# Linear attention, a Fourier mix and an MLP on one core: every engine's order written by a list scheduler of the kernel's own

## The chip, the cores and the metric

The kernel runs on one core of a Trainium2 chip. A core has five engines that run at the same time, each taking its own instructions strictly in the order in which they stand: TensorE (PE, matmuls), VectorE (DVE), ScalarE (ACT), GpSimd (POOL) and SyncE (SP, which here only issues transfers). Engines wait for one another through semaphores; transfers run on 16 DMA engines that all queues share. The metric is the device time of one execution in microseconds, as the median of several runs.

## The reference

Inputs are r, k, v of 4 batches x 8 heads x 768 steps x 48, a decay w and a bonus u of 8 x 48, and two MLP weights. The output is 4 x 768 x 384 in float32.

```python
for t in range(S):                       # linear attention, per batch and head
    cur = u*k_t (outer) v_t
    y_t = r_t @ (state + cur)
    state = w*state + k_t (outer) v_t
x = y, heads side by side                # (4, 768, 384)
mixed = real(fft(fft(x, axis=1), axis=2))
u = x + mixed
un = (u - mean(u)) / sqrt(var(u) + 1e-06)
out = u + relu(un @ w_ch1) @ w_ch2       # 384 -> 1536 -> 384
```

## The kernel before

A batch has six chunks of 128 steps, so there are 24 chunks (numbered 0 to 23), one Fourier transform a batch, and 8 half batches of 384 rows (hf 0 to 7) for the MLP.

**A chunk** takes three phases. `phase1`: k and r (tile kr) times powers of the decay give KR on DVE; v is cast to V on ACT; PE turns KR (eight transposes into tp), ACT copies that to KRT, and DVE multiplies its halves into PR. `phase2`: eight score matmuls A_ps; the triangle mask gives MA, either by a cast AC on ACT and a select on POOL, or by one multiplication on DVE; u_ps is the state's update, which DVE scales into Sst. `phase3`: yd_ps collects the bonus, the state's part and the chunk's own part; ACT copies the bonus out (DE), POOL multiplies it with V (TT), DVE adds the two into X.

**A batch** whose X is complete is folded by `fold` (EO, XF on DVE) and transformed by `fourier`: 18 matmuls over time (L298) whose results ACT casts into TT2 (called TT in the trace's rows, L300), DVE reverses them into TR, then six blocks of six matmuls over columns (L316 to L320), to which DVE adds X (UF) and of which it takes mean and variance (st, MV). ACT takes the root (rstd), DVE inverts it and makes nm, ACT writes the normed rows UN, and a transposing DMA on SP's queue turns them into UNT (L339). The MLP is `mlp1` (12 pieces of three matmuls and a Relu on ACT into HT) and `mlp2` (three pieces of twelve matmuls, the addition osb on DVE, and the output's DMA issued by POOL). All of this shares eight PSUM banks, three of them the ring "mm" of the transforms and the MLP.

**The order** is that of a hand-written loop over 26 steps: it calls phase1 of chunk s, phase2 of chunk s - 1, phase3 of chunk s - 2, and between them steps the transform in hand (`advance`) and takes from the list M of MLP pieces (`feed`). The framework's own scheduler then moves instructions on each engine by its estimates, except those held by `keep_in_program_order` (all of SP's). Six chunks of inputs are loaded ahead; the tables te, to and hid come behind them. W1 and W2 are loaded by POOL's queue after the TT of chunks 2 and 6 (`marks`).

Of the kernel before, what the change touches and what calls it, by code (L numbers as in the profile page):

```python
# [9 lines left out]
AluOp = mybir.AluOpType  # L10
# [16 lines left out]
def _tables():  # L27
# [31 lines left out]
    return [np.ascontiguousarray(x.astype(bf)) for x in (te, to, hid, mtri, ident)]  # L59


@with_exitstack
def kernel(
# [106 lines left out]

    def load(i):
        b, q = divmod(i, NQ)
        sl = slice(q * 128, (q + 1) * 128)
        kr = inp.tile([128, 2, H, D], F32, name="kr")
        vt = inp.tile([128, H, D], F32, name="vt")
        sp(nc.sync.dma_start(out=kr[:, 0], in_=k[b, :, sl, :].rearrange("h p d -> p h d")))  # L176
        sp(nc.sync.dma_start(out=kr[:, 1], in_=r[b, :, sl, :].rearrange("h p d -> p h d")))
        if i == 0:
            sp(nc.sync.dma_start(out=ident, in_=id_c.ap()))
        sp(nc.sync.dma_start(out=vt, in_=v[b, :, sl, :].rearrange("h p d -> p h d")))  # L180
        if i == 0:
            sp(nc.sync.dma_start(out=mtri, in_=mtri_c.ap()))
        chk[i]["in"] = (kr, vt)


    def phase1(i):
        c = chk[i]
        kr, vt = c["in"]
        KR = KRs[i % NB]
        nc.vector.tensor_tensor(  # L190
            out=KR.rearrange("t s p (a d) -> t (s p) a d", a=2)[:, :, :, 0:D],
            in0=kr.rearrange("t s (p a) d -> t (s p) a d", a=2),
            in1=wtab.rearrange("t s (p a d) -> t (s p) a d", a=2, d=D), op=AluOp.mult)
        V = wp.tile([128, H, D], BF16, name="V", bufs=4)
        cv = nc.scalar.copy(V, vt)  # L195
        if i == 0:
            tc.keep_in_program_order(cv)
        tp = ps.tile([128, 2, NP, 128], BF16, name="tp", bufs=1)
        for s in range(2):
            for p in range(NP):  # L200
                nc.tensor.transpose(tp[:, s, p, :], KR[:, s, p, :], ident)  # L201
        KRT = wp.tile([128, 2, NP, 128], BF16, name="KRT", bufs=4)
        nc.scalar.copy(KRT, tp)  # L203
        PR = wp.tile([128, NP, 128], BF16, name="PR", bufs=4)
        nc.vector.tensor_tensor(out=PR, in0=KRT[:, 0], in1=KRT[:, 1], op=AluOp.mult)  # L205
        c.update(KR=KR, V=V, KRT=KRT, PR=PR)

    def phase2(i):
        b, q = divmod(i, NQ)
        c = chk[i]  # L210
        KR, V, KRT = c["KR"], c["V"], c["KRT"]
        A_ps = [ps.tile([128, NP, 128], F32, name="A_ps", bufs=2) for _ in range(2)]
        for p in range(NP):
            for a in range(2):
                rows = slice(a * 64, a * 64 + 64)
                nc.tensor.matmul(A_ps[a][:, p, :], lhsT=KRT[rows, 0, p, :], rhs=KRT[rows, 1, p, :],  # L216
                                 start=(p == 0), stop=(p == NP - 1), skip_group_check=True)
        MAs = []
        for a in range(2):
            MA = wp.tile([128, NP, 128], BF16, name="MA", bufs=6)  # L220
            if a == 0 and b > 0:
                nc.vector.tensor_tensor(out=MA, in0=A_ps[a], in1=mtri.unsqueeze(1).to_broadcast([128, NP, 128]),
                                        op=AluOp.mult)
            else:
                AC = wp.tile([128, NP, 128], BF16, name="AC", bufs=2)
                nc.scalar.copy(AC, A_ps[a])  # L226
                nc.gpsimd.affine_select(out=MA, in_=AC, pattern=[[0, NP], [1, 128]], base=0,  # L227
                                        channel_multiplier=-1, compare_op=AluOp.is_gt, fill=0.0)
            MAs.append(MA)
        S = c.get("S")  # L230
        if q < NQ - 1:
            u_ps = ps.tile([128, NP, 2, D], F32, name="u_ps", bufs=1)
            for p in range(NP):
                nc.tensor.matmul(u_ps[:, p, :, :], lhsT=KR[:, 0, p, :], rhs=V[:, 2 * p:2 * p + 2, :],
                                 start=(p == 0), stop=(q == 0 and p == NP - 1), skip_group_check=True)
            if q > 0:
                nc.tensor.matmul(u_ps, lhsT=ident, rhs=S, start=False, stop=True, skip_group_check=True)
            Sn = wp.tile([128, NP, 2, D], BF16, name="Sst", bufs=4)
            nc.vector.tensor_tensor(out=Sn, in0=u_ps, in1=WD, op=AluOp.mult)
            chk[i + 1]["S"] = Sn  # L240
        c["MA"] = MAs
# [215 lines left out]
```

## Time and profile before

| | |
|---|---|
| runs | 235.19 us median of 3 (232.9 to 235.21) |
| the profiled execution | 235.22 us; its span, from first to last instruction, 233.5 us |
| busy share of the span | PE 82%, DVE 56%, ACT 55%, POOL 27% |
| TensorE's granted clock, mean | 0.931 of full speed |
| read from memory | 20.32 MB, of which k, r, v in pieces of 192 bytes |

The profile page divides the span into 40 equal slices and gives each engine's busy tenths in each. PE's line reads 2 to 9 with dips; the DMA line reads 9 from the second to the 16th slice and little behind that. A busy PE is not a PE at its peak: its durations double when its clock is at the lower level, and a row of the page does not say what an instruction waits for in a queue.

### The profile page before, as it was taken

How to read it: one execution, taken by the hardware profiler on the slowest of the kernel's cores; microseconds unless marked ns; L12 is line 12 of the kernel's file. 1: busy time of each engine (PE TensorE's matmuls, PEld its weight loads, DVE VectorE, ACT ScalarE, POOL GpSimd, SP SyncE). 2: the span in 40 equal slices, each digit the busy share in tenths (PEclk: the TensorE clock that was granted, in tenths of full speed). 3: DMA queues.
4: the chain of work that ended last, by engine and by line, in shares of the span. 5: the costliest groups of instructions: out<-in, count | busy, mean ns of one | idle time of the engine just before them, and what ended most of it. 6: DMA issues, size and time to landing. Idle time of an engine off the chain costs nothing.

```text
span 233.5 us, 4269 instructions
## 1 busy us (share of the span) xinstructions
PE 191.2 (82%) x1640; PEld 122.3 (52%) x1640; DVE 131.1 (56%) x273; ACT 129.3 (55%) x261; POOL 64.1 (27%) x93
## 2 busy tenths in 40 slices
PE   0289856991798979987999789964999999999990
PEld 0156634670555645665565456652565565566660
DVE  4367479795955694598881454782841277101020
ACT  4677534734798675577247564543356637654500
POOL 4038944701213441343100133162001000101021
PEclk9999999999599988995599999995699999999998
DMA  5999999999999996101603940102003103310111
GB/s 108 187 188 197 284 206 186 181 190 190 175 177 166 208 182 137 36 0 36 121 34 66 210 70 10 36 34 53 0 34 84 36 34 86 84 70 35 67 70 67
DMA packets 88917, 25.33 MB, mean 108 GB/s; under 512 B 85312, under 2 KB 86976, under 8 KB 88896
## 3 DMA queue, kind: packets, MB, share of 16 engines
q1 hardware_dynamic: 85216, 17.96, 44.7%
q0 software_dynamic: 3680, 7.08, 11.8%
q8 instruction: 13, 0.21, 0.4%
q14 instruction: 8, 0.07, 0.1%
HBM read 20.32 MB, written 4.72 MB: 107 GB/s over the span
## 4 chain that ended last, share of the span: by engine, by line
issue 29%; PE 22%; ACT 11%; DMA 11%; POOL 9%; DVE 8%; SPq 6%; POOLq 0%; ACTq 0%; DVEq 0%
PE mm L353 6%; PE mm L362 5%; DMA vt<-in_v_dram 5%; DMA kr<-in_r_dram 5%; POOL TT L264 4%; POOL out_dram L367 3%; ACT KRT L203 3%; PE tp L201 3%; ACT HT L355 2%; ACT UN L337 2%; POOL MA L227 2%; SPq L176 2%; PE mm L298 2%; PE A_ps L216 2%; DMA UNT<-UN 2%
## 5 line engine op out<-in xcount | busy, mean ns | idle before, releaser
L355 ACT ACTIVATE HT<-mm 128x384 bf16<-128x384 f32 x96 | 46.0, 497 | 35.1 <-PE mm L353 34.7
L353 PE MATMUL mm<-UNT,W 128*128 128x384 bf16 x288 | 59.2, 341 | 2.7 <-DMA UNT<-UN 1.7
L362 PE MATMUL mm<-W,HT 128*128 128x384 bf16 x288 | 51.4, 331 | 0.0
L353 PEld LDWEIGHTS <-W 128*128 128x128 bf16 x288 | 28.3, 101 | 21.2 <-issue 4.8
L362 PEld LDWEIGHTS <-HT 128*128 128x128 bf16 x288 | 28.6, 99 | 19.5 <-issue 1.6
L365 DVE TENSOR_TENSOR osb<-mm,UF 128x384 f32<-128x384 f32 x24 | 13.4, 557 | 43.2 <-PE mm L362 43.1
L367 POOL DMA_DIRECT2D out_dram<-osb x24 | 13.3, 555 | 87.9 <-DVE osb L365 87.9
L227 POOL TENSOR_SCALAR_AFFINE_SELECT MA<-AC 128x512 bf16<-128x512 bf16 x30 | 22.2, 751 | 40.1 <-ACT AC L226 35.5
L264 POOL TENSOR_TENSOR TT<-V,DE 128x384 bf16<-128x384 bf16 x24 | 22.6, 941 | 36.4 <-ACT DE L262 34.2
L190 DVE TENSOR_TENSOR KR<-kr,wtab 128x768 bf16<-128x768 f32 x24 | 23.7, 991 | 12.9 <-DMA kr<-in_r_dram 12.9
L201 PE MATMUL tp<-ident,KR 128*128 128x128 bf16 x192 | 20.0, 258 | 12.3 <-DVE KR L190 11.5
L203 ACT COPY KRT<-tp 128x1024 bf16<-128x1024 bf16 x24 | 24.3, 1012 | 7.7 <-PE tp L201 7.3
L201 PEld LDWEIGHTS <-KR 128*128 128x128 bf16 x192 | 15.0, 116 | 15.4 <-DVE KR L190 13.4
L216 PE MATMUL A_ps<-KRT 64*128 64x128 bf16 x192 | 15.4, 257 | 9.0 <-ACT KRT L203 4.4
L226 ACT CAST AC<-A_ps 128x512 bf16<-128x512 f32 x30 | 17.2, 592 | 9.9 <-PE A_ps L216 9.8
L271 DVE TENSOR_TENSOR X<-yd_ps,TT 128x384 bf16<-128x384 f32 x24 | 13.3, 553 | 14.8 <-POOL TT L264 14.4
L195 ACT CAST V<-vt 128x384 bf16<-128x384 f32 x24 | 12.4, 515 | 12.6 <-POOL TT L264 6.6
L300 ACT CAST TT<-mm 128x386 bf16<-128x386 f32 (+1 forms) x24 | 14.1, 603 | 5.6 <-PE mm L298 5.5
L337 ACT ACTIVATE UN<-UF,nm,rstd 128x384 bf16<-128x384 f32 x24 | 15.2, 697 | 3.6 <-DVE nm L333 3.5
L216 PEld LDWEIGHTS <-KRT 64*128 64x128 bf16 x192 | 8.5, 108 | 15.5 <-issue 7.4
L205 DVE TENSOR_TENSOR PR<-KRT 128x512 bf16<-128x512 bf16 x24 | 11.3, 471 | 8.5 <-ACT KRT L203 8.4
L269 PE MATMUL yd_ps<-V,MA 128*128 128x48 bf16 x192 | 11.0, 199 | 5.3 <-ACT DE L262 3.5
(64 smaller groups left out, 239.7 us busy)
## 6 DMA issues: line engine op xcount, KB each, us to landing
kr<-in_k_dram SPq DMA_DIRECT2D x24, 192.0 KB, 4.6
kr<-in_r_dram SPq DMA_DIRECT2D x24, 192.0 KB, 4.6
vt<-in_v_dram SPq DMA_DIRECT2D x24, 192.0 KB, 4.7
out_dram<-osb POOLq DMA_DIRECT2D x24, 192.0 KB, 2.2
W<-in_moe_w_ch_dram POOLq DMA_DIRECT2D x6, 384.0 KB, 7.6
hid_t<-hid_c SPq DMA_DIRECT2D x1, 576.0 KB, 5.7
te_t<-te_c SPq DMA_DIRECT2D x1, 289.5 KB, 4.8
to_t<-to_c SPq DMA_DIRECT2D x1, 288.0 KB, 4.5
```

Of the source, the lines that this page charges most:

```text
L190: nc.vector.tensor_tensor(out=KR.rearrange("t s p (a d) -> t (s p) a d", a=2)[:, :, :, 0:D], in0=kr.rearrange("t s (p a) d -> t (s p) a d" ...
L201: nc.tensor.transpose(tp[:, s, p, :], KR[:, s, p, :], ident)
L203: nc.scalar.copy(KRT, tp)
L216: nc.tensor.matmul(A_ps[a][:, p, :], lhsT=KRT[rows, 0, p, :], rhs=KRT[rows, 1, p, :], start=(p == 0), stop=(p == NP - 1), skip_group_check ...
L226: nc.scalar.copy(AC, A_ps[a])
L227: nc.gpsimd.affine_select(out=MA, in_=AC, pattern=[[0, NP], [1, 128]], base=0, channel_multiplier=-1, compare_op=AluOp.is_gt, fill=0.0)
L264: marks[i] = nc.gpsimd.tensor_tensor(out=TT, in0=V, in1=DE.unsqueeze(2).to_broadcast([128, H, D]), op=AluOp.mult)
L337: nc.scalar.activation(out=UN[:, j, :], in_=UF[:, j, :], func=Act.Identity, scale=rstd[:, j:j + 1], bias=nm[:, j:j + 1])
L353: nc.tensor.matmul(hp, lhsT=W1[:, dt, ft * 128:(ft + 1) * 128], rhs=UNT[:, :, dt, :], start=(dt == 0), stop=(dt == 2))
L355: nc.scalar.activation(out=HTs[hf][:, ft, :], in_=hp, func=Act.Relu)
L362: nc.tensor.matmul(op, lhsT=HTs[hf][:, ft, j * 128:(j + 1) * 128], rhs=W2[:, ft, :], start=(ft == 0), stop=(ft == 11))
L367: nc.gpsimd.dma_start(out=out[b, row:row + 128, :], in_=osb)
```

## The change

The loop, `feed` and `advance` go. In their place every operation (a group of matmuls, a cast, a DMA) is declared with an engine, a duration in nanoseconds, what it reads and writes, and a priority; `_Schedule.order` then plays a clock over them, always taking next the operation that can start first, with rings of buffers and one serial DMA pipe among the conditions; and `emit` writes the instructions in that order, which `manual_schedule` keeps. The operations themselves stay, with these exceptions.

- The normed rows of batch 0 are turned by PE (18 transposes against ident into the ring mm) and copied to UNT by DVE; batches 1 to 3 keep the DMA.
- kr and vt have rings of 4 buffers where they had 6, AC 3 where it had 2.
- Chunk 5 too has one of its masks on DVE now, and a chunk's POOL mask is made ahead of its DVE mask.
- `mlp2` is two operations of six matmuls, between which others may stand. W1 and W2 are issued behind the start of TT of chunks 3 and 7.

The diff, cut to its core (what was a loop body is the same instruction inside `op`):

```diff
+    LATENCY = 80
+    LANDING = 1900
+    COLD = 42000
...
+        def room(o):
+            t = 0.0
+            taken = {}
+            for tl in o["new"]:
+                ring = rings.setdefault(tl.ring, [])
+                n = len(ring) + taken.get(tl.ring, 0) - tl.bufs
+                taken[tl.ring] = taken.get(tl.ring, 0) + 1
+                if n >= 0:
+                    if n >= len(ring):
+                        return None
+                    for p in ring[n].ops:
+                        if "end" not in p:
+                            return None
+                        t = max(t, p["end"])
...
+            for e, ops in cand.items():
+                at = free.get(e, 0.0)
+                pick = None
+                for o in ops:
+                    t = room(o)
+                    if t is None:
+                        continue
+                    start = max(at, o["ready"], t + self.LATENCY)
+                    key = (start, o["pri"], o["n"])
+                    if pick is None or key < pick[0]:
+                        pick = (key, o)
+                if pick and (best is None or pick[0] < best[0]):
+                    best = pick
+            assert best, "no operation can start"
+            (start, _, _), o = best
+            cand[o["eng"]].remove(o)
+            ns = o["ns"] * (1.9 if o["eng"] == "PE" and start < self.COLD else 1)
+            end = start + ns
+            free[o["eng"]] = end
+            if o["dma"]:
+                dma_free = max(dma_free, end) + o["dma"]
+                end = dma_free + self.LANDING
+            o["start"], o["end"] = start, end
+            for tl in o["new"]:
+                rings[tl.ring].append(tl)
+            done.append(o)
...
+        c["kr"] = kr = new(inp, [128, 2, H, D], F32, "kr", 4)
+        c["vt"] = vt = new(inp, [128, H, D], F32, "vt", 4)
+        op("SP", 600, lambda: nc.sync.dma_start(out=kr()[:, 0], in_=k[b, :, sl, :].rearrange("h p d -> p h d")),
+           w=[("k", i)], new=[kr], dma=1030, pri=10 * i - 50)
...
+        op("ACT", 510, lambda: nc.scalar.copy(V(), vt()), r=[("v", i), "wtab"], w=[("V", i)], new=[V], use=[vt], pri=pri + 1)
...
+            if a == 0 and i >= NQ - 1:
...
+        for a in (1, 0):
+            mask(a)
...
+            if b == 0:
+                for j in range(3):
+                    turned(sh, j, UN, UNT)
+                op("NONE", 0, lambda: None, r=[("UNT", b, sh, j) for j in range(3)], w=[("UNT", b, sh)])
+                return
+            op("SP", 1200, lambda: nc.sync.dma_start_transpose(
+                out=UNT().rearrange("p j c t -> p (j c) t"), in_=UN().rearrange("p j d -> p (j d)")),
+               r=[("UN", b, sh, j) for j in range(3)], w=[("UNT", b, sh)], new=[UNT], use=[UN], dma=1500, pri=-1000)
+
+        def turned(sh, j, UN, UNT):
+            tq = new(ps, [128, 3, 128], BF16, "mm", 3)
+
+            def mm():
+                for dt in range(3):
+                    nc.tensor.transpose(tq()[:, dt, :], UN()[:, j, dt * 128:(dt + 1) * 128], ident)
+
+            op("PE", 200, mm, r=[("UN", b, sh, j)], w=[("tq", sh, j)], new=[tq], use=[UN], pri=pri + 1 + sh)
+            op("DVE", 450, lambda: nc.vector.tensor_copy(UNT()[:, j, :, :], tq()), r=[("tq", sh, j)],
+               w=[("UNT", b, sh, j)], new=[UNT] if j == 0 else [], use=[tq, UNT],
+               after=[("UNT", b, sh, 0)] if j else [], pri=-100)
+
+        for sh in range(2):
+            UF = new(bp, [128, 3, DM], F32, "UF", 5)
+            UNT = new(bp, [128, 3, 3, 128], BF16, "UNT", 5)
...
+        op("PE", 985, lambda: mm(0, 6), r=[("HT", hf, ft) for ft in range(6)] + ["W2"], w=[("mo", hf, j, 0)], new=[mo],
+           use=[HT], pri=pri)
+        op("PE", 985, lambda: mm(6, 12), r=[("HT", hf, ft) for ft in range(6, 12)] + [("mo", hf, j, 0)],
+           w=[("mo", hf, j)], use=[HT, mo], pri=pri)
...
+    weights("W1", lambda n: w1[n * 128:(n + 1) * 128, :], lambda n: W1[:, n, :], [("TT", 3)])
+    weights("W2", lambda n: w2[n * 512:(n + 1) * 512, :].rearrange("(f p) d -> p f d", p=128),
+            lambda n: W2[:, n * 4:(n + 1) * 4, :], [("TT", 7)])
...
+    with tc.manual_schedule():
+        sch.emit()
```

Three places show what the scheduler makes of it. In the rows a name's number tells one buffer from another.

ACT at the start of the program, before and then after; lw, wtab, lwc and wdec are the tables of the decay's powers, V the cast of chunk 0 (vt_122, vt_127 its input), KRT the copy of its turned rows:

```order
L113 ACTIVATE lw_90<-wrow_71 128x384
L116 ACTIVATE wtab_92<-lw_90,icol_77 128x384
L115 ACTIVATE wtab_92<-lw_90,ncol_79 128x384
L118 ACTIVATE lwc_95<-wuc_81 128x4
L120 ACTIVATE wdec_97<-lwc_95 128x4
L121 ACT_TABLE_LOAD
L195 CAST V_157<-vt_122 128x384
L203 COPY KRT_168<-tp_159 128x1024
```

```order
L239 ACTIVATE lw_90<-wrow_71 128x384
L319 CAST V_143<-vt_127 128x384
L242 ACTIVATE wtab_92<-lw_90,icol_77 128x384
L241 ACTIVATE wtab_92<-lw_90,ncol_79 128x384
L244 ACTIVATE lwc_95<-wuc_81 128x4
L246 ACTIVATE wdec_97<-lwc_95 128x4
L247 ACT_TABLE_LOAD
L327 COPY KRT_165<-tp_146 128x1024
```

The cast of chunk 0's v, which followed the tables and the second table load, now stands ahead of wtab.

ACT from the last casts TT2 of batch 0's transform to its first normed rows, before and then after; V_631, V_781 and V_894 are the casts of chunks 8 to 10, V_654 and V_678 those of chunks 8 and 9, AC, DE and KRT belong to chunks 7 to 9, rstd and UN to the half batch hf 0:

```order
L300 CAST TT2_651<-mm_693 128x2x192
L195 CAST V_631<-vt_367 128x384
L300 CAST TT2_651<-mm_699 128x386
L203 COPY KRT_642<-tp_633 128x1024
L300 CAST TT2_651<-mm_704 128x2x192
L195 CAST V_781<-vt_439 128x384
L226 CAST AC_860<-A_ps_848 128x512
L262 COPY DE_880<-yd_ps_871 128x8
L195 CAST V_894<-vt_512 128x384
L203 COPY KRT_792<-tp_783 128x1024
L330 ACTIVATE rstd_770<-MV_736,eps_t_88 128x3
L337 ACTIVATE UN_775<-UF_734,nm_773,rstd_770 128x384 x3
```

```order
L467 CAST TT2_633<-mm_525 128x386
L319 CAST V_654<-vt_395 128x384
L467 CAST TT2_633<-mm_646 128x2x192
L467 CAST TT2_633<-mm_657 128x386
L319 CAST V_678<-vt_464 128x384
L467 CAST TT2_633<-mm_668 128x2x192
L327 COPY KRT_701<-tp_680 128x1024
L350 CAST AC_786<-A_ps_767 128x512
L398 COPY DE_798<-yd_ps_777 128x8
L521 ACTIVATE rstd_810<-MV_726,eps_t_88 128x3
L327 COPY KRT_812<-tp_788 128x1024
L530 ACTIVATE UN_823<-UF_722,nm_817,rstd_810 128x384 x3
```

Before, the casts of chunks 9 and 10 and one KRT stand between the last TT2 and rstd; now the casts of chunks 8 and 9 stand among the TT2, and ahead of rstd there is one KRT and no cast, with another KRT between rstd and UN.

DVE behind the transform of batch 1, up to nm of hf 2, before and then after; UF, st and MV lead to rstd and nm of hf 2 and hf 3, osb is the MLP's output, the rest (X, PR, MA, Sst) is attention:

```order
L326 BN_AGGR MV_1517<-st_1561 128x2
L205 TENSOR_TENSOR PR_1627<-KRT_1625 128x512
L325 BN_STATS st_1594<-UF_1515 128x6
L222 TENSOR_TENSOR MA_1668<-A_ps_1658,mtri_74 128x512
L326 BN_AGGR MV_1517<-st_1594 128x2
L239 TENSOR_TENSOR Sst_1680<-u_ps_1674,WD_100 128x384
L331 RECIPROCAL rstd_1597<-rstd_1597 128x3
L271 TENSOR_TENSOR X_1357<-yd_ps_1714,TT_1725 128x384
L333 SCALAR_TENSOR_TENSOR nm_1600<-MV_1517,rstd_1597 128x3
```

```order
L505 TENSOR_TENSOR UF_1624<-mm_1626,X_659 128x2x192
L510 BN_STATS st_1666<-UF_1529 128x6
L512 BN_AGGR MV_1578<-st_1666 128x2
L510 BN_STATS st_1678<-UF_1624 128x6
L512 BN_AGGR MV_1692<-st_1678 128x2
L510 BN_STATS st_1696<-UF_1624 128x6
L523 RECIPROCAL rstd_1690<-rstd_1690 128x3
L602 TENSOR_TENSOR osb_1706<-mm_1668,UF_756 128x384
L525 SCALAR_TENSOR_TENSOR nm_1708<-MV_1578,rstd_1690 128x3
```

Before, three attention operations (MA, Sst, X) stand between the last st of hf 2 and its nm; now one osb of the MLP does, and two st of hf 3.

## Rows read from the trace of the kernel before

**Rows 1.** Timeline: start, duration, engine, line; first MLP matmuls (PE), last addition (DVE).

```profile
63.73 1.16 PE L353 MATMUL mm<-UNT,W 128*128 128x384 bf16 x3
...
228.30 0.56 DVE L365 TENSOR_TENSOR osb<-mm,UF 128x384 f32<-128x384 f32 x1 [1.39 <-PE mm L362]
```

**Rows 2.** Waiting chain in order of time: start, duration; matmul groups at the full clock.

```profile
76.30 1.95 PE mm L362 x12
...
147.80 0.33 PE A_ps L216 x8
...
152.95 0.46 PE tp L201 x8
```

**Rows 3.** PE's groups from 63.7 on: line, shapes, count, busy us, mean ns.

```profile
L201 PE MATMUL tp<-ident,KR 128*128 128x128 bf16 x104 | 9.5, 228 | 1.0 <-ACT KRT L203 0.6 <-DVE KR L190 0.3
```

**Rows 4.** Windows of 4 us: busy PE, PEld, DVE, ACT, POOL; PEclk; DMA share, GB/s.

```profile
60.00:64.00 4.00, 3.42 (x39) 2.37 (x37) 3.55 (x8) 2.74 (x7) 1.42 (x2) 0.50 0.88 163
...
104.00:108.00 4.00, 2.41 (x27) 1.78 (x28) 3.74 (x10) 3.13 (x6) 1.79 (x3) 0.74 0.00 2
108.00:112.00 4.00, 3.38 (x45) 2.66 (x42) 3.47 (x6) 2.73 (x7) 2.15 (x3) 0.50 0.50 92
112.00:116.00 4.00, 3.86 (x20) 2.17 (x17) 2.92 (x6) 0.49 (x1) 0.28 (x1) 0.50 0.73 136
...
156.00:160.00 4.00, 1.12 (x22) 0.90 (x19) 2.07 (x5) 2.54 (x5) 1.53 (x3) 0.64 0.00 0
160.00:164.00 4.00, 2.38 (x25) 1.44 (x22) 1.49 (x3) 0.17 (x1) 1.44 (x2) 0.50 0.41 78
164.00:168.00 4.00, 4.00 (x20) 2.35 (x19) 3.50 (x7) 1.47 (x3) 0.00 (x0) 0.58 0.00 0
```

**Rows 5.** ACT's timeline from 44 to 64 us; in brackets idle time and what ended it.

```profile
55.04 0.51 ACT L195 CAST V<-vt 128x384 bf16<-128x384 f32 x1 [3.16 <-DMA vt<-in_v_dram]
...
56.36 0.30 ACT L330 ACTIVATE rstd<-MV,eps_t 128x3 f32<-128x3 f32 x1
57.62 1.90 ACT L337 ACTIVATE UN<-UF,nm,rstd 128x384 bf16<-128x384 f32 x3 [0.96 <-DVE nm L333]
```

**Rows 6.** DVE's timeline: the third mean and variance of hf 0.

```profile
52.88 0.17 DVE L326 BATCH_NORM_AGGREGATE MV<-st 128x2 f32<-128x6 f32 x1
```

**Rows 7.** SP's timeline (issue of the first transposing DMA) and tile UNT's landing times.

```profile
59.55 1.39 SPq L339 DMA_TRANSPOSE UNT<-UN  x1
...
DMA to landing us min/median/max: 3.2/3.4/4.7
```

**Rows 8.** Groups by line: reversing copy and addition on DVE, 128 partitions.

```profile
L322 DVE TENSOR_TENSOR UF<-mm,X 128x384 f32<-128x384 f32 x24 | 13.0, 547 | 3.2 <-PE mm L320 3.1
...
L302 DVE COPY TR<-TT 128x768 bf16<-128x768 bf16 x12 | 4.8, 402 | 8.0 <-ACT TT L300 7.9
```

**Rows 9.** Timeline: chunk 9's v, issued by SP, and batch 0's last TT2 cast.

```profile
41.40 0.83 SPq L180 DMA_DIRECT2D vt<-in_v_dram  x1
...
47.33 0.62 ACT L300 CAST TT<-mm 128x384 bf16<-128x384 f32 x1
```

**Rows 10.** DMA, three issues of v (4.56, 41.40, 44.22 us): KB, us to landing.

```profile
vt<-in_v_dram SPq DMA_DIRECT2D x1, 192.0 KB, 3.6
...
vt<-in_v_dram SPq DMA_DIRECT2D x1, 192.0 KB, 6.4
...
vt<-in_v_dram SPq DMA_DIRECT2D x1, 192.0 KB, 10.7
```

**Rows 11.** Timelines of ACT and DVE at the program's start.

```profile
5.22 0.61 ACT L116 ACTIVATE wtab<-lw,icol 128x384 f32<-128x384 f32 x1
...
7.09 0.96 DVE L190 TENSOR_TENSOR KR<-kr,wtab 128x768 bf16<-128x768 f32 x1 [3.28 <-DMA kr<-in_r_dram]
```

**Rows 12.** DVE's timeline behind batch 1's transform, and PE's first matmuls of hf 2.

```profile
106.29 0.47 DVE L333 SCALAR_TENSOR_TENSOR nm<-MV,rstd 128x3 f32<-128x3 f32 x1
...
112.79 1.12 PE L353 MATMUL mm<-UNT,W 128*128 128x384 bf16 x3
```

More of the change, by code (lines that the diff above doesn't have):

```diff
@@ L181, in load @@
         if i == 0:
[L182 to L206, printed above, removed]
@@ L208, in phase2, with attend @@
-    def phase2(i):
+            op("SP", 400, lambda: nc.sync.dma_start(out=mtri, in_=mtri_c.ap()), w=["mtri"], dma=100, pri=-46)
+    def attend(i):
         b, q = divmod(i, NQ)
         c = chk[i]
[L211 to L229, printed above, removed]
@@ new lines, in attend, with scores @@
+        op("DVE", 410, lambda: nc.vector.tensor_tensor(out=PR(), in0=KRT()[:, 0], in1=KRT()[:, 1], op=AluOp.mult),
+           r=[("KRT", i)], w=[("PR", i)], new=[PR], use=[KRT], pri=pri + 1)
+        A_ps = [new(ps, [128, NP, 128], F32, "A_ps", 2) for _ in range(2)]
+        MA = [new(wp, [128, NP, 128], BF16, "MA", 6) for _ in range(2)]
+        def scores():
+            for p in range(NP):
+                for a in range(2):
+                    rows = slice(a * MASKROWS, (a + 1) * MASKROWS)
+                    nc.tensor.matmul(A_ps[a]()[:, p, :], lhsT=KRT()[rows, 0, p, :], rhs=KRT()[rows, 1, p, :],
+                                     start=(p == 0), stop=(p == NP - 1), skip_group_check=True)
@@ new lines, in first @@
+                y = yd()[:, 0:DM].rearrange("t (h d) -> t h d", h=H)
+                for p in range(NP):
+                    nc.tensor.matmul(y[:, 2 * p:2 * p + 2, :], lhsT=KRT()[:, 1, p, :], rhs=S()[:, p, :, :],
+                                     start=False, stop=False, skip_group_check=True)
+        op("PE", 115 + (170 if q else 0), first, r=[("PR", i), "WD"] + ([("S", i)] if q else []), w=[("de", i)],
+           new=[yd], use=[PR, KRT] + ([S] if q else []), pri=pri + 1)
+        op("ACT", 180, lambda: nc.scalar.copy(DE(), yd()[:, DM:]), r=[("de", i)], w=[("DE", i)], new=[DE], use=[yd], pri=pri)
@@ L357, in mlp2, with mm @@
-    def mlp2(hf, j):
+            HTs[hf] = new(bp, [128, 12, 384], BF16, "HT", 3)
+        HT = HTs[hf]
+        hp = new(ps, [128, 384], F32, "mm", 3)
+        def mm():
+            for dt in range(3):
+                nc.tensor.matmul(hp(), lhsT=W1[:, dt, ft * 128:(ft + 1) * 128], rhs=UNT()[:, :, dt, :],
+                                 start=(dt == 0), stop=(dt == 2))
+        op("PE", 495, mm, r=[("UNT", hf // 2, hf % 2), "W1"], w=[("hp", hf, ft)], new=[hp], use=[UNT], pri=pri)
+        op("ACT", 490, lambda: nc.scalar.activation(out=HT()[:, ft, :], in_=hp(), func=Act.Relu), r=[("hp", hf, ft)],
+           w=[("HT", hf, ft)], new=[HT] if ft == 0 else [], use=[hp, HT], after=[("HT", hf, 0)] if ft else [], pri=-100)
```

450 lines of the change are left out of this document (273 added, 177 removed).

## The prediction

> **What bounds the kernel now.** I first look for where the matmuls that no order can avoid begin and end. The MLP is more than half of all matmul work, and its first one runs at 63.73 us; the last addition on DVE starts at 228.30, right behind the last matmul [rows 1], and 5.2 us of span (233.5) are left for it, its output transfer and the end. So the span is a start of 63.7, a middle of 164.6 and a tail of 5.2, and the profiled execution took 1.7 us more than its span (235.22, which is the median of the runs within 0.03).
>
> How much of the middle is work? Twelve MLP matmuls at the full clock take 1.95 us, 0.163 each [rows 2]. All 576 lie there: 93.6. Of the transforms of batches 1 to 3 there are 54 time matmuls at the same price, 8.8, and 18 column blocks, each worth four full widths, 11.7. Attention still has 104 turns [rows 3], 13 chunks, at 0.46 a chunk, as many scores at 0.33 [rows 2], 15 chunks' own parts that I price as scores (5.0), some 150 small matmuls at 0.04, and 8 wide ones (7.5 together): 22.8. Sum 136.9, so 27.7 us of the middle are lost. PE is the bound by its work, and order decides about the rest.
>
> The windows say where two large losses are [rows 4]. From 104 to 116 PE idles 2.35 us, and its granted clock is 0.74, 0.50, 0.50, so that of its busy 2.41, 3.38 and 3.86 us some 4.25 are the price of the lower level (1.2 GHz for 2.4): 6.6 in all. From 156 to 168 the same sum gives 4.5 idle and 3.3 by the clock, 7.8. Both lie where a half batch's normed rows were not ready and no MLP piece was left to run. The other 13.3 us are gaps of a microsecond or two and waits inside groups that count as busy.
>
> Then I read the start backwards from 63.73. UNT comes from a transposing DMA issued at 59.55, landing 3.2 to 4.7 us later [rows 7]. Its input UN starts at 57.62, and rstd before it at 56.36 [rows 5]. But the third mean and variance was done by 53.05 [rows 6]. The 3.3 us between are ACT's: it stood 3.16 us at the cast of chunk 10's v, whose transfer was in flight together with W2 and took 10.7 us where the first such one took 3.6 [rows 5, 10].
>
> **The change: the start.** In the new order no cast of chunk 10 stands ahead of rstd, and W2 is issued later, behind TT of chunk 7. What is late next is DVE's own chain, which the new order makes about as long (three additions of hf 1 come in, a KR goes out): I take the third variance at 53.5, rstd at 53.6 to 53.9, nm at 54.3. On ACT a KRT of about one microsecond stands between rstd and UN, so UN starts at 54.9 and ends at 56.8 (1.90, rows 5). In place of the DMA come three transposes and a copy for each third of a half batch. Eight turns take 0.46 [rows 2], so three take 0.17. The copy of 128x384 out of PSUM has no row: a reversing copy of twice the size out of SBUF takes 0.40, an addition of that size that reads PSUM 0.55 [rows 8]; I take 0.47, nearer the second, which also reads PSUM, and a gain below zero is excluded, since the copy is added work. With two hand-overs the last third ends 0.9 behind UN: MLP from 57.7 or 57.8 instead of 63.73. Two other waits could take this place. The last TT2 is now behind the cast of chunk 9, whose v was issued at 41.40 [rows 9] and landed 6.4 later beside W2 [rows 10]; without W2 I take 3.6 to 6.4, that is 45.0 to 47.8, and two casts behind it end at 46.1 to 48.9, against 47.95 before [rows 9]. And V of chunk 0 now stands ahead of wtab: it waits for its input until 4.56 + 3.6 = 8.2 [rows 10], and the first KR, at 7.09 before, comes at about 9.9 [rows 11]. I cost these 2.8 us at nothing, because batch 0 ends with the inputs' landing, not with its first chunk; without that cover they would be added whole.
>
> The 18 transposes cost PE 18 x 0.06 = 1.0 us, half of them behind the first MLP matmul. The Trainium skill prices them higher: "TensorE: Matmul & The Clock Gate", Part 4, gives about 275 ns for one 128x128 transpose in a kernel and notes that its result needs a copy out of PSUM. By that the 18 would take 5.0 us and the forecast would be some 3 us later; the trace's turns, eight in 0.46 us [rows 2], do not agree when they stand in a row, and I go by the trace.
>
> **The change: the middle.** Counting the new order, behind its first MLP matmul stand the same MLP and transforms, 14 turns, 15 scores, 16 own parts and 9 of the turned rows' transposes: 136.9 + 2.5 = 139.4. Its losses I take from the old ones. The hole at 156 goes (7.8): between the last column block of batch 2 and the first matmul of hf 4 the new order has 13.8 us of other PE work, against a chain of additions, norm and transfer of about 11. Of the hole at 104, 2.5 of 6.6 stay. There nm came at 106.29 and the first matmul of hf 2 at 112.79 [rows 12]; now 36 matmuls of mlp2 (5.9 us) and two chunks' attention (2.1) stand between the last column block and hf 2, but one osb that waits for twelve of those matmuls stands ahead of nm on DVE. From that block: 0.9 for the rest of an own part and the scores, 1.95 and 0.55 for the osb, 0.2 for nm, 1.9 for UN, 3.4 for the DMA, 0.5 for hand-overs make 9.4 against 8.0, 1.4 idle and as much again should the clock fall. New is a slow beginning: from 52 on PE has little to do in both orders, and the clock then was at 0.50 in 60 to 64 [rows 4], where there was little to slow down; now about 5 us of MLP work meet it, 2.5. Of the other 13.3 I take a third off, 4, since pieces of 0.3 to 1 us are now placed one by one, and not more, because ACT has as much to do as PE between the MLP's start and the transform of batch 1. Losses: 27.7 - 7.8 - 4.1 + 2.5 - 4 = 14.3.
>
> The tail keeps its 5.2: mlp2 pieces, osb, transfer, as before. The smaller rings, the third AC buffer, the mask of chunk 5 and the split of mlp2 I count inside those losses.
>
> Sum: 57.8 + 139.4 + 14.3 + 5.2 = 216.7 of span, with 1.7 around it **218.4**, I say 218.
>
> **The rivals.** *Late and cold* (0.16): the column blocks of batch 0 still run at the lower clock, since PE has waited for chunk 6's v just before, or chunk 9's v lands late; twelve blocks' worth is then 3.9 us longer, the MLP starts at 61.7 and runs at the lower level some 3 us longer: 224. For it speaks that u_ps of chunk 6 now stands on PE ahead of chunk 5's own part; against it that before, too, the clock rose in time. *No better in the middle* (0.16): the list's clock has all transfers in one pipe and knows no contention, so that an engine stands at the wrong instruction as often as the old order did; losses stay at 27.7: 232. *Better* (0.10): all but half of the small gaps vanish and the clock never falls: 211. *The other side* (0.06): casts of V stand on ACT ahead of Relus and DE, and with 4 instead of 6 buffers their loads can't run ahead; each of the 14 remaining chunks then holds ACT and so PE. At w us each the time is 218 + 14 w; it passes 235 from w = 1.2, and at 2 it is 246. One cast waited 3.16 even with six buffers [rows 5]; against it speaks that the DMA share is near zero at 104 and 156 [rows 4], so that a load issued then lands quickly. That the order isn't the declared one is seen in one place, V ahead of wtab, and its price is in the sum.
>
> **The numbers.** My forecast has 0.52. Its own losses, 10 to 18, and the start, 56 to 60, make 213 to 223. To leave out no more than 2 in 10 the range takes in *better* and *late* and some of *no better*: 209 to 230. A difference of 1% (2.35 us) is about what a measurement of this kernel can tell from none. Faster by more: 0.52 + 0.16 + 0.10 and two thirds of *no better*, 0.89; within 1%: 0.05; slower by more: 0.06.
>
> **What would show it.** In the profile after: the first MLP matmul at 56 to 60 us, with rstd right behind the third variance; no window in the 150s with PE under 3 of 4 us; a hole of 1 to 3 us before hf 2; the granted clock at 0.5 once, around the MLP's start, and a mean of about 0.95 or more; the last matmul some 17 us earlier. Wrong would be: several stops of ACT at V behind DMA, a clock that falls at each transform, or a start behind 62.

## The result, and the profile after

The changed kernel takes 211.84 us (median of 4 runs, 209.63 to 214.71) where the kernel before took 234.46 in the same job: ratio 0.901, 95% interval 0.892 to 0.911. The forecast was 218 in a range of 209 to 230. One of the experiments, loads_real, beats both kernels at 204.95 us. The profiled execution of the changed kernel was a disturbed one (214.71 us, span 213.0, mean clock 0.948, where the other spans were 207.9 to 210.2); sizes are therefore read a second time from the same kernel run again, after_again below (211.81 us; its profiled span is 208.2 at clock 0.984).

The timeline of the changed kernel, its first MLP matmuls on PE and its last addition on DVE, as in [rows 1]:

```profile
59.60 3.04 PE L579 MATMUL mm<-UNT,W 128*128 128x384 bf16 x9 [0.45 <-DVE UNT L554]
...
207.69 0.56 DVE L602 TENSOR_TENSOR osb<-mm,UF 128x384 f32<-128x384 f32 x1 [1.39 <-PE mm L595]
```

So the start, up to the first MLP matmul, is 59.6 (63.7 before), the middle 148.1 (164.6), the tail 5.3 (5.2). Most of the gain lies in the middle. One window over it, and the windows that answer to [rows 4] (busy PE, PEld, DVE, ACT, POOL; PEclk; DMA share, GB/s):

```profile
59.60:207.69 148.09, 144.38 (x1285) 93.23 (x1284) 92.61 (x191) 97.74 (x200) 39.99 (x55) 0.96 0.44 89
...
60.00:64.00 4.00, 4.00 (x20) 1.71 (x19) 2.26 (x6) 2.06 (x4) 0.17 (x1) 0.50 1.30 200
...
104.00:108.00 4.00, 3.13 (x41) 2.07 (x39) 3.65 (x10) 3.12 (x7) 1.43 (x3) 1.00 0.87 169
108.00:112.00 4.00, 1.95 (x7) 0.92 (x7) 4.00 (x6) 1.09 (x3) 1.25 (x2) 0.61 0.91 179
112.00:116.00 4.00, 4.00 (x48) 3.01 (x47) 1.24 (x3) 2.39 (x5) 0.83 (x1) 0.54 1.34 186
...
156.00:160.00 4.00, 4.00 (x27) 2.42 (x26) 1.60 (x4) 3.55 (x8) 0.54 (x1) 1.00 0.13 49
160.00:164.00 4.00, 4.00 (x39) 3.16 (x37) 3.25 (x7) 0.37 (x1) 0.00 (x0) 1.00 0.02 4
```

PE idles 3.7 us of the middle where it idled 13.7. As 2.9 of them lie before hf 2, from 107 to 110, no second hole like that at 156 is left. Behind the hole before hf 2 the clock is at the lower level (1.2 GHz). Its rows on DVE, SP and PE:

```profile
101.93 0.56 DVE L602 TENSOR_TENSOR osb<-mm,UF 128x384 f32<-128x384 f32 x1 [0.29 <-PE mm L595]
102.40 0.15 DVE L525 SCALAR_TENSOR_TENSOR nm<-MV,rstd 128x3 f32<-128x3 f32 x1
...
104.52 4.60 SPq L542 DMA_TRANSPOSE UNT<-UN  x2
...
110.05 2.08 PE L579 MATMUL mm<-UNT,W 128*128 128x384 bf16 x6 [2.63 <-DMA UNT<-UN]
```

As forecast, nm stands behind an osb; but UNT then takes 5.5 us to land, where [rows 7] had 3.4. In flight beside it are outputs of the MLP and the transfer of hf 3; one load of v had landed at 104.05, the next was issued at 109.21. Which of these makes it longer was not tried. The start, on ACT:

```profile
41.05 0.51 ACT L319 CAST V<-vt 128x384 bf16<-128x384 f32 x1 [4.90 <-DMA vt<-in_v_dram]
...
46.84 0.51 ACT L319 CAST V<-vt 128x384 bf16<-128x384 f32 x1 [1.14 <-DMA vt<-in_v_dram]
47.26 0.58 ACT L467 CAST TT<-mm 128x384 bf16<-128x384 f32 x1
...
54.25 0.30 ACT L521 ACTIVATE rstd<-MV,eps_t 128x3 f32<-128x3 f32 x1
...
55.67 1.90 ACT L530 ACTIVATE UN<-UF,nm,rstd 128x384 bf16<-128x384 f32 x3 [0.22 <-DVE nm L525]
```

No cast of V stands between the last TT2 and rstd now [rows 5]; two others stop ACT earlier, at the v of chunks 7 and 9. Counted in order, the cast at 41.05 is the eighth, so it is chunk 7's; the expectations of after_again, gates_510 and times_37 call it chunk 6's, whose cast started at 33.39 without a wait. Chunk 7's v was issued at 30.24 and took 10.7 us. What it shared the DMA engines with is told by the rows of the queues (packets, MB, share): from 14 to 22 us loads alone, and then from 30 to 38, with W1 in POOL's queue (q0).

```profile
q1 hardware_dynamic: 7801, 1.47, 136.8%
...
q0 software_dynamic: 428, 1.17, 77.9%
q1 hardware_dynamic: 2301, 0.44, 30.4%
```

In 8 us the loads, in packets of some 190 bytes, fall from 1.47 to 0.44 MB beside W1's packets of 2.7 KB. The Trainium skill, "DMA: Bandwidth & Descriptors", section "Queues, rings and completion order", says that a DMA engine takes turns between the rows of queues, one whole packet at a time. The trace agrees in so far as the queue of long packets gets most of the bytes (1.17 of 1.61 MB). It shows some five short packets for each long one, and not the turns themselves, nor whether what the profile counts as a packet is one of that page's packets.

### The profile page after: what moved, and what is told of

Its sections match the earlier page's. It is cut to its first block, busy times and chain, and to the rows that moved or that the text cites. A ratio compares the mean times of both kernels' runs of the same rounds, so it can differ in the third digit from the quotient of the medians.

```text
span 213.0 us, 4295 instructions
## 1 busy us (share of the span) xinstructions
PE 180.6 (85%) x1658; PEld 118.5 (56%) x1658; DVE 134.1 (63%) x280; ACT 130.0 (61%) x260; POOL 64.6 (30%) x92
## 3 DMA queue, kind: packets, MB, share of 16 engines
q0 software_dynamic: 3680, 7.08, 13.3%
## 4 chain that ended last, share of the span: by engine, by line
PE 35%; issue 26%; DMA 11%; DVE 9%; POOL 8%; ACT 6%; SPq 2%; POOLq 0%; ACTq 0%
PE mm L579 10%; DMA vt<-in_v_dram 9%; PE mm L595 6%; PE tp L324 4%; POOL out_dram L605 4%; POOL MA L352 3%; PE A_ps L338 3%; PE mm L460 3%; DVE KR L314 3%; DMA UNT<-UN 3%; PE yd_ps L408 2%; PE mm L495 2%; POOL TT L399 2%; DVE st L510 1%; ACT AC L350 1%
## 5 line engine op out<-in xcount | busy, mean ns | idle before, releaser
L583 ACT ACTIVATE HT<-mm 128x384 bf16<-128x384 f32 x96 | 45.9, 493 | 26.3 <-PE mm L579 26.2
L579 PE MATMUL mm<-UNT,W 128*128 128x384 bf16 x288 | 55.9, 340 | 3.4 <-DMA UNT<-UN 2.6
L595 PE MATMUL mm<-W,HT 128*128 128x384 bf16 x288 | 50.4, 326 | 0.0
L602 DVE TENSOR_TENSOR osb<-mm,UF 128x384 f32<-128x384 f32 x24 | 13.3, 555 | 40.5 <-PE mm L595 40.2
L399 POOL TENSOR_TENSOR TT<-V,DE 128x384 bf16<-128x384 bf16 x24 | 21.6, 899 | 46.2 <-ACT DE L398 39.0
L352 POOL TENSOR_SCALAR_AFFINE_SELECT MA<-AC 128x512 bf16<-128x512 bf16 x29 | 23.6, 822 | 37.1 <-ACT AC L350 21.4
L605 POOL DMA_DIRECT2D out_dram<-osb x24 | 13.3, 556 | 60.0 <-DVE osb L602 55.1
L314 DVE TENSOR_TENSOR KR<-kr,wtab 128x768 bf16<-128x768 f32 x24 | 25.4, 1073 | 8.9 <-ACT wtab L241 5.9
L324 PE MATMUL tp<-ident,KR 128*128 128x128 bf16 x192 | 18.6, 254 | 12.0 <-DVE KR L314 10.7
L350 ACT CAST AC<-A_ps 128x512 bf16<-128x512 f32 x29 | 16.5, 588 | 13.4 <-PE A_ps L338 13.1
L412 DVE TENSOR_TENSOR X<-yd_ps,TT 128x384 bf16<-128x384 f32 x24 | 13.1, 546 | 7.8 <-POOL TT L399 7.6
L467 ACT CAST TT<-mm 128x386 bf16<-128x386 f32 (+1 forms) x24 | 12.8, 599 | 3.0 <-PE mm L460 2.8
L345 DVE TENSOR_TENSOR MA<-A_ps,mtri 128x512 bf16<-128x512 f32 x19 | 12.9, 678 | 2.7 <-PE A_ps L338 2.7
L505 DVE TENSOR_TENSOR UF<-mm,X 128x384 f32<-128x384 f32 x24 | 12.5, 548 | 1.8 <-PE mm L499 1.3
L373 DVE TENSOR_TENSOR Sst<-u_ps,WD 128x384 bf16<-128x384 f32 x20 | 11.0, 551 | 3.7 <-PE u_ps L366 1.8
```

Source lines behind the costliest of these rows:

```text
L314: op("DVE", 960, lambda: nc.vector.tensor_tensor(out=KR().rearrange("t s p (a d) -> t (s p) a d", a=2)[:, :, :, 0:D], in0=kr().rearrange(" ...
L324: nc.tensor.transpose(tp()[:, s, p, :], KR()[:, s, p, :], ident)
L350: op("ACT", 590, lambda: nc.scalar.copy(AC(), A_ps[a]()), r=[("A", i)], w=[("AC", i, a)], new=[AC], use=[A_ps[a]], pri=pri)
L352: op("POOL", 680, lambda: nc.gpsimd.affine_select(out=MA[a](), in_=AC(), pattern=[[0, NP], [1, 128]], base=0, channel_multiplier=-1, compa ...
L399: op("POOL", 850, lambda: nc.gpsimd.tensor_tensor(out=TT(), in0=V(), in1=DE().unsqueeze(2).to_broadcast([128, H, D]), op=AluOp.mult), r=[( ...
L579: nc.tensor.matmul(hp(), lhsT=W1[:, dt, ft * 128:(ft + 1) * 128], rhs=UNT()[:, :, dt, :], start=(dt == 0), stop=(dt == 2))
```

## The experiments

Each kernel was timed in three rounds beside the kernel before (median 235.27, 234.79 and 235.03 in the three groups of four experiments). "Behind it" counts the chunks whose eight turns tp stand behind the first MLP matmul; busy and idle are PE's between that and the last osb, in each kernel's profiled execution.

| kernel | us | ratio, 95% interval | MLP from | middle | busy | idle | behind it |
|---|---|---|---|---|---|---|---|
| before | 235.2 | | 63.73 | 164.6 | 150.9 | 13.7 | 13 |
| after_again | 211.81 | 0.893 to 0.913 | 58.18 | 144.7 | 141.1 | 3.7 | 14 |
| turn_dma | 213.62 | 0.903 to 0.923 | 72.47 | 133.9 | 132.6 | 1.3 | 10 |
| gates_510 | 210.69 | 0.890 to 0.906 | 59.95 | 142.4 | 140.4 | 2.1 | 14 |
| fw_sched | 222.85 | 0.939 to 0.959 | 64.43 | 149.0 | 142.6 | 6.4 | 14 |
| before_parts | 241.19 | 1.022 to 1.036 | 68.80 | 164.3 | 147.5 | 16.9 | 11 |
| flat | 239.79 | 1.017 to 1.027 | 71.29 | 161.9 | 148.8 | 13.1 | 13 |
| turn_all | 208.75 | 0.884 to 0.897 | 58.46 | 142.0 | 140.8 | 1.2 | 14 |
| loads_real | 204.95 | 0.868 to 0.881 | 58.31 | 139.8 | 138.6 | 1.2 | 13 |
| times_37 | 208.88 | 0.882 to 0.893 | 56.37 | 144.2 | 141.3 | 2.8 | 15 |
| gates_68 | 206.12 | 0.873 to 0.881 | 56.42 | 142.7 | 141.6 | 1.2 | 14 |
| real_turn | 207.27 | 0.878 to 0.887 | 57.59 | 141.7 | 140.0 | 1.7 | 13 |
| unsplit | 208.45 | 0.884 to 0.899 | 57.87 | 142.3 | 140.1 | 2.3 | 14 |

**after_again**, nothing edited.

> The changed kernel once more, unaltered, for a second profile. Theory: its first MLP matmul stands again at 59 to 60 us behind two waits of ACT at V (about 5 us for chunk 6, about 1 us for chunk 9), and before hf 2 PE again idles 1.5 to 3 us for UNT's transfer; time 209 to 213 us, ratio 0.89 to 0.91. Rival: these waits belonged to that one execution (its clock was lower than in the others); then one or both are gone here and the start is below 57.

The two waits of ACT (3.7 us at chunk 7's v, 1.6 at chunk 9's) and the hole of 2.6 us before hf 2 come back: they are the kernel's own. The start is 58.2, and the granted clock is 1.00 there, so the slow beginning does not belong to every execution.

**turn_dma.**
```diff
-            if b == 0:
+            if False:
                 for j in range(3):
                     turned(sh, j, UN, UNT)
```

> Batch 0's normed rows go through the transposing DMA again, all else as changed, planned anew by the list. Theory: the turn on TensorE is worth what the transfer takes less the three copies, so the first MLP matmul comes 2 to 4 us later (62 to 64), and since PE has attention's work to fill part of it, the end comes 1 to 3 us later: 213 to 215. Rival 1: the turn is the whole gain of the start and more, 216 to 218. Rival 2: the transfer is hidden by other PE work, within 1 us of the changed kernel.

The time moved as expected, by 1.8 us (the intervals overlap, but all four times lie above all of after_again), though not for the reason given: the MLP starts 14.3 us later, not 2 to 4. UNT takes 8.3 and 10.7 us to land beside loads and W2, and in the new order PE does four chunks' turns and more meanwhile, so that only 10 are left behind the start and the middle is 10.8 us shorter. The windows from the span's start to the first MLP matmul, in before, after_again, turn_dma and loads_real (columns as in [rows 4]):

```profile
0.00:63.73 63.73, 40.27 (x420) 27.92 (x421) 43.54 (x97) 36.12 (x68) 27.60 (x40) 0.96 1.08 190
...
0.00:58.18 58.18, 35.05 (x373) 24.26 (x374) 40.65 (x91) 31.91 (x60) 24.00 (x36) 0.97 1.15 191
...
0.00:72.47 72.47, 46.30 (x511) 33.51 (x512) 53.60 (x111) 42.25 (x78) 30.91 (x44) 0.84 1.17 188
...
0.00:58.31 58.31, 37.70 (x395) 26.35 (x395) 42.91 (x93) 33.83 (x64) 23.26 (x35) 0.97 1.12 190
```

In a start 14.3 us longer than that of after_again PE idles only 3.1 us more (26.2 for 23.1), and 2.3 less behind it. What the late start costs is mostly the clock: it is at 0.50 from 60 to 72 us, where after_again has 1.00 from 58 on. By windows of 1 us (busy time times what the clock lacks) I estimate its price in the start at 8.7 us, for 1.5 in after_again. The issue of both transfers on SP, and their landing:

```profile
56.89 8.01 SPq L542 DMA_TRANSPOSE UNT<-UN  x2
...
DMA to landing us min/median/max: 8.3/9.5/10.7
```

**before_parts** (the kernel before, with two parts of the change).
```diff
-            sp(nc.sync.dma_start_transpose(...
+            if b == 0:
+                for j in range(3):
+                    tq = ps.tile([128, 3, 128], BF16, name="mm", bufs=3)
+                    for dt in range(3):
+                        nc.tensor.transpose(tq[:, dt, :], UN[:, j, dt * 128:(dt + 1) * 128], ident)
+                    nc.vector.tensor_copy(UNT[:, j, :, :], tq)
...
-            if s - 2 == 2:
+            if s - 2 == 3:
...
-            if s - 2 == 6:
+            if s - 2 == 7:
```

> The kernel before, with its hand-written loop and the framework's order, and two parts of the change alone: batch 0's normed rows turned on TensorE, and W1 and W2 issued behind TT of chunks 3 and 7. Theory: the order carries nearly all of the gain, and these two only move the MLP's start by some 3 us, of which the middle gives part back: 232 to 234 (ratio 0.985 to 1.0). Rival: they are worth the start as I summed it, 6 us: 228 to 230 (0.97 to 0.98).

Both were wrong: it is 2.9% slower than before. On DVE the last copy to UNT of hf 0 is done by 57.98; on PE the MLP's first matmul comes at 68.80:

```profile
57.34 0.64 DVE L344 COPY UNT<-mm 128x384 bf16<-128x384 bf16 x2
...
66.85 0.50 PE L343 MATMUL mm<-ident,UN 128*128 128x128 bf16 x3 [1.85 <-ACT UN L337]
...
68.80 1.49 PE L360 MATMUL mm<-UNT,W 128*128 128x384 bf16 x4
```

Between them stand the column blocks of hf 1, attention, and the transposes of hf 1, for which PE waits for ACT. A wait that SP's queue took before now stands in PE's own queue, ahead of the MLP. ACT itself had stood 1.99 us at a cast of V just ahead of that UN. The two parts were not tried apart, so what the moved weights have in the loss is open. In this order the turned rows do not pay; in the list's order, which puts the MLP ahead of hf 1's transposes, they are worth the 1.8 us of turn_dma.

**fw_sched.**
```diff
-    with tc.manual_schedule():
-        sch.emit()
+    sch.emit()
```

> The same operations written in the list's order, but the framework's scheduler may move them by its own estimates (the order is not held). Theory: what the middle gained is the order by measured times, which the framework undoes in part: losses in the middle go back up by 5 to 15 us, 217 to 227. Rival: the written order alone does it, because the framework moves little; then within 2 us of the changed kernel.

The theory holds in time (11.0 us slower than after_again), less so in place: 6.3 of the 10.4 us between the two spans are the start (64.43), 4.3 the middle. Against before, the list's order, even when moved, keeps half the gain. The hand-written loop with its own order held was not run; flat, next, is held too and slower than before, so holding an order does not by itself make the gain.

**flat.**
```diff
+        ns = 600 if ns else 0
         o = dict(eng=eng, ns=ns, ...
```

> The list scheduler with one duration, 600 ns, for every operation in place of the measured ones; priorities, rings, transfers and dependences as changed. Theory: the measured durations decide where an operation fits, and with wrong ones PE stands in front of results that are not ready: at least 8 us slower, 220 to 240. Rival: interleaving by priority and buffers alone does it, and the engines' own waits correct the rest: 211 to 215.

The theory holds: 28 us slower than the changed kernel, and slower than the hand-written loop. PE idles 13.1 us behind a start at 71.29. With this one duration the list is worth nothing; the gain comes with the measured ones. The rings, the third AC and the mask of chunk 5 are in flat as well, so they do not make the gain by themselves.

**gates_510.**
```diff
-    weights("W1", lambda n: w1[n * 128:(n + 1) * 128, :], lambda n: W1[:, n, :], [("TT", 3)])
+    weights("W1", lambda n: w1[n * 128:(n + 1) * 128, :], lambda n: W1[:, n, :], [("TT", 5)])
...
-            lambda n: W2[:, n * 4:(n + 1) * 4, :], [("TT", 7)])
+            lambda n: W2[:, n * 4:(n + 1) * 4, :], [("TT", 10)])
```

> W1 is issued behind TT of chunk 5 and W2 behind TT of chunk 10 (changed kernel: 3 and 7). Theory: the start is held by chunk 6's v, which is 10.7 us in flight beside W1; without W1 it lands by 36 instead of 41, ACT's wait at V shrinks from 4.9 to under 1.5 us, the MLP starts at 55 to 57 and the time falls 2 to 4 us, to 208 to 210. Rival: the loads of chunks 6 to 9 are late whatever else is in flight, or W1 itself becomes the last; then the start stays at 59 to 60 or goes later and the time stays at 211 to 214.

The theory falls: the start is 59.95, later than in after_again, as in the rival. The time, 1.1 us less and within the intervals, lies between both bets. Chunk 7's v now comes in time (its cast starts at 34.39 without a wait); but W1, issued at 35.36, meets chunk 9's, and the last TT2 casts stand behind its cast:

```profile
46.68 0.51 ACT L319 CAST V<-vt 128x384 bf16<-128x384 f32 x1 [4.44 <-DMA vt<-in_v_dram]
47.10 1.03 ACT L467 CAST TT<-mm 128x386 bf16<-128x386 f32 x2
```

**turn_all.**
```diff
-            if b == 0:
+            if b <= 1:
...
-            op("PE", 200, mm, r=[("UN", b, sh, j)], w=[("tq", sh, j)], new=[tq], use=[UN], pri=pri + 1 + sh)
+            op("PE", 200, mm, r=[("UN", b, sh, j)], w=[("tq", b, sh, j)], new=[tq], use=[UN], pri=pri + 1 + sh)
```

> Batch 1's normed rows too are turned on TensorE (18 transposes and 6 copies more), so that hf 2 does not wait for a transfer of 5.4 us. Theory: the hole of 2.6 us before hf 2 and the lower clock behind it go, for 1.1 us more of PE: 1.5 to 3 us faster than the changed kernel, 209 to 210.5. Rival: hf 2 then starts earlier but PE misses the same work later, since what is lost is set by how much PE work there is beside ACT and DVE; within 1 us of 211.8, or slower by the copies on DVE.

The theory holds, with a little more than expected: 3.1 us less than after_again, with intervals that just overlap. The start is the same (58.46), PE's idle time falls from 3.7 to 1.2, its clock in the middle is 1.00.

**loads_real** (both loads of kr as that of vt).
```diff
-        op("SP", 600, lambda: nc.sync.dma_start(out=vt(), in_=v[b, :, sl, :].rearrange("h p d -> p h d")),
+        op("SP", 1000, lambda: nc.sync.dma_start(out=vt(), in_=v[b, :, sl, :].rearrange("h p d -> p h d")),
...
-            op("POOL", 700, lambda n=n: nc.gpsimd.dma_start(out=dst(n), in_=src(n)), after=gate, w=[(name, n)], dma=1900,
+            op("POOL", 700, lambda n=n: nc.gpsimd.dma_start(out=dst(n), in_=src(n)), after=gate, w=[(name, n)], dma=2600,
...
-    weights("W1", lambda n: w1[n * 128:(n + 1) * 128, :], lambda n: W1[:, n, :], [("TT", 3)])
+    weights("W1", lambda n: w1[n * 128:(n + 1) * 128, :], lambda n: W1[:, n, :], [("TT", 6)])
...
-            lambda n: W2[:, n * 4:(n + 1) * 4, :], [("TT", 7)])
+            lambda n: W2[:, n * 4:(n + 1) * 4, :], [("TT", 8)])
```

> The list is told what the trace shows of loads: 1000 ns for an issue on SP (it had 600), 2600 for a third of a weight (1900), and W1 and W2 go behind TT of chunks 6 and 8. Theory: no V cast stands on ACT ahead of its data for more than 1.5 us, since the loads of chunks 6 to 9 no longer share the DMA engines with W1; the MLP starts at 54 to 56 and the time falls by 2 to 4 us to 208 to 210. Rival: an earlier MLP start buys little, because PE only does the MLP instead of attention then (the run with the transfer for batch 0 lost 1.8 us at the end for a start that was 14 us later): under 1 us, 211 to 212.

More than expected, 6.9 us less than after_again, the fastest of all: ratio 0.874 to before. No V cast of chunks 6 to 9 stops ACT. Yet the start did not move (58.31), so the part of the theory that wanted it at 54 to 56 falls. What moved is the work ahead of it: one chunk more is done there, and PE idles 20.6 us for 23.1 (the windows under turn_dma). Behind it PE idles 1.2 for 3.7, and there is no hole before hf 2 (UNT lands in 3.2 to 3.9). These two, some 2.5 us each, make up the 4.9 us between the profiled spans.

```profile
58.31:198.11 139.80, 138.57 (x1265) 90.26 (x1263) 90.15 (x187) 95.01 (x197) 42.13 (x57) 1.00 0.48 95
```

**times_37**, the first two pieces of that diff alone.

> Of loads_real the load times alone (1000 ns an issue on SP, 2600 a third of a weight), with the weights behind TT of chunks 3 and 7 as in the changed kernel. Theory: what helps is where W1 goes, so that it doesn't share the DMA engines with chunks 6 to 9; with the old places V of chunk 6 waits again for some 4 us and the time is 210 to 212. Rival: the truer load times alone put the V casts where their data are, whenever W1 comes: 205 to 207.

**gates_68**, the last two pieces alone.

> Of loads_real the places of the weights alone (behind TT of chunks 6 and 8), with the load times as changed. Theory: W1 out of the way of chunks 6 to 9 gives most of the gain, 205 to 208. Rival: with the short load times the list still puts casts ahead of data that come later, and ACT stands as it did with chunks 5 and 10: 210 to 211.

The places of the weights carry most: gates_68 lies within the interval of loads_real, and its theory holds. It shows, too, that a wait of ACT need not cost: a cast of V stands 5.90 us, up to 50.40, but behind the last TT2. The load times alone give 2.9 us, between both bets: but for chunk 0's all casts are in time, and the start is the earliest of all (56.37). PE idles 2.8 us behind it, 1.3 of them at 103, behind the first matmuls of hf 2, where attention waits for X on DVE.

**real_turn**, the diffs of loads_real and turn_all together.

> loads_real and batch 1's normed rows turned on TensorE too. Theory: in loads_real PE is busy for 138.6 of the 139.8 us behind the MLP's start, so no hole is left before hf 2; 18 transposes more cost 1 us: 205 to 206.5. Rival: the gain of 3 us that the turn brought to the changed kernel adds to that of the loads: 202 to 203.

Both bets are missed, the rival by more. The two gains do not add, since the hole that the turn removes is not there. At 207.27 it costs 2.3 us, more than the 1 us of transposes, with intervals that overlap; where the rest goes was not taken apart.

**unsplit.**
```diff
-        op("PE", 985, lambda: mm(0, 6), r=[("HT", hf, ft) for ft in range(6)] + ["W2"], w=[("mo", hf, j, 0)], new=[mo],
...
+        op("PE", 1970, lambda: mm(0, 12), r=[("HT", hf, ft) for ft in range(12)] + ["W2"], w=[("mo", hf, j)], new=[mo],
```

> The changed kernel with mlp2 in pieces of twelve matmuls (it has two of six). Theory: the split is worth little, since PE's idle time behind the start is 3.7 us and nearly all of it one hole before hf 2: 210 to 213. Rival: smaller pieces are what lets attention's operations in at the right time; without them PE and the buffers of mm are held 2 us at a time: 214 to 217.

Both were wrong: it is 3.4 us less than after_again by the medians, with intervals that just overlap. Without the split nm of hf 2 stands ahead of the osb, and PE does not wait for UNT there; that this is the whole difference is not shown, as the list is planned anew:

```profile
95.88 0.16 DVE L525 SCALAR_TENSOR_TENSOR nm<-MV,rstd 128x3 f32<-128x3 f32 x1
...
96.38 0.56 DVE L600 TENSOR_TENSOR osb<-mm,UF 128x384 f32<-128x384 f32 x1 [0.25 <-PE mm L595]
```

## Why the prediction was right, and where it was off

The direction and the mechanism held: order was what could be gained, PE's work behind the first MLP matmul was counted right, and the time is that work plus its losses. I had 139.4 of work; busy at the full clock are 140.8 in turn_all, with 1.0 us more of transposes, and 138.6 in loads_real, with a chunk less. But 211.84 lies below my forecast's own 213 to 223. The number is nearly that of the *better* rival (211), to which I gave 0.10, but not its mechanism: there half of the small gaps stay and the clock never falls, while here nearly all of them went and the clock was at the lower level twice in the middle of the profiled execution, once in that of after_again.

- **The losses were mis-sized**, and this is the term of the sum that was furthest off: "Of the other 13.3 I take a third off, 4". Losses of 14.3 were forecast; the middle less 139.4 gives 8.7 in the profiled execution and 5.3 in after_again. In the first, the windows give 2.4 for the slow beginning (I had 2.5) and 2.9 idle with 2.8 of clock around hf 2, so that less than 1 us is left of 13.3. What the 13.3 were can be read from windows of the trace before, outside the two holes: PE idles 6.8 us, the lower clock costs an estimated 2.3, and the other 4 lie in groups that count as busy. In after_again PE idles 0.8 us outside the hole before hf 2, at the full clock. The small gaps went almost whole; that ACT had as much to do as PE was no bound. That the measured durations took them away is what flat shows: without them PE idles 13.1 us in the middle.
- **The hole before hf 2 was too small**: 2.5 forecast, 5.7 measured in the profiled execution. Its form was right (an osb ahead of nm), the transfer was not: 5.5 us, where I took 3.4 from [rows 7].
- **The hole at 156** went, 7.8, as forecast.
- **The start** was 59.6, or 58.2 in after_again, for 57.8. rstd at 54.25 and 53.33 (forecast 53.6 to 53.9) and UN at 55.67 and 54.75 (54.9) came within 0.8 us; the last TT2 ended within the bounds named, held by chunk 9's v as I had feared. The third transposes came late: an own part, which waited 0.31 us for a mask on DVE, and eight scores stood ahead of them on PE. So UNT was whole 2.0 us behind UN (1.5 in after_again) and not 0.9.
- **W1** I left out; late loads stand under *late and cold* alone. It was in flight beside chunk 7's v. Chunk 9's was issued at 42.45, when W1 had landed, so that its lateness is that of SP's queue. With both weights later (gates_68) the start comes 1.8 us earlier and the time falls by 5.7; the hole before hf 2 is gone there too.
- **Turned rows**: the copy takes 0.35 (I took 0.47, nearer an addition), and the transposes are as cheap as KR's. Their group on PE (count, busy us, mean ns of one):

```profile
L551 PE MATMUL mm<-ident,UN 128*128 128x128 bf16 x18 | 2.1, 234 | 0.6 <-ACT UN L530 0.6
```

One lasts 234 ns, but they overlap, and 18 keep PE busy for 2.1 us, part of them at the lower clock; I had 1.0. The 275 ns that the Trainium skill gives for one ("TensorE: Matmul & The Clock Gate", Part 4) are near the duration of one here. The 5.0 us worked out from them for 18 do not come.
- **V of chunk 0 ahead of wtab**: the first KR starts at 9.71 (forecast 9.9). That this costs nothing was not tried by itself.
- **That the start is 6 us of gain** was too simple. Ahead of the MLP PE idles 23.5 us before and 23.1 in after_again: the earlier start is work moved behind it, and what is gained is the middle's idle time (13.7 to 3.7) and its lower clock (an estimated 9.9 to 1.4). turn_dma gives 14.3 us of start away for 1.8 of time, and before_parts has the turned rows and loses: what the start gains is decided by what PE does in it.
- **The other side** (V casts on ACT with 4 buffers) did not come: of 9.8 us that ACT stood ahead of V in the whole program, 9.1 were for the transfers of v, in three stops ahead of the MLP. I had named several such stops as a sign of being wrong; they came, but ahead of the MLP, where the start still lay in the range named.
- **The split of mlp2**, counted inside the losses, seems to be a loss itself.
- **Two slips** of the working changed nothing: what I name as new in the middle's work adds up to 2.0 and not 2.5, and batch 0 has six column blocks and not twelve (the 3.9 us are right for six).

## What to carry to other kernels

Where one engine is the bound, add up its work behind the first point that no order can avoid, and treat everything else as loss; here a list order brought PE's idle time behind that point from 13.7 us to 3.7, and with better load times and places to 1.2, so don't keep a share of the old ones without naming what holds them. An order written from a model is as good as the model's durations, and the ones that were off here were those of transfers that meet others: give the list the issue time and the landing that the trace shows under load, and keep big transfers away from the small ones that an in-order engine waits for. A wait behind which PE also runs at the lower clock costs more than its length. A step moved onto the bound's engine helps only if what waits for it stands close behind it and its own wait stands in front of nothing.

## What the runs showed of the hardware

- A transposing DMA of 384 rows landed in 3.2 us at the least, in 5.5 beside outputs of the MLP, and in 8.3 to 10.7 beside loads and weights (turn_dma).
- An issue on SP mostly took 0.4 to 0.6 us in the first 5 us and about 1.0 where loads were issued one behind another; one beside W1 took 5.1, the two transposes of turn_dma 8.0 together.
- The mean granted clock of one program differed between executions without ordering their spans: 0.992 with a span of 210.1, 0.970 with 207.9.
